# Attention and gated long convolution on one core: a new order for every engine's work, with higher planned costs for the shared-key loads

## The chip, the core and the metric

The kernel runs on one core of a Trainium2 chip. Its metric is the device time in microseconds, from the start of the program to its end. The three timed runs of the kernel before took 371.93, 372.42 and 373.16 us (median 372.42). A profile of one more execution was taken with the hardware profiler.

A core has five engines that each work through their own list of instructions: TensorE (PE, matmuls; its weight loads are listed apart as PEld), VectorE (DVE), ScalarE (ACT), GpSimd (POOL) and SyncE (SP, which here only issues transfers). An engine that waits for a semaphore holds up all that stands behind in its list.

## The reference

```python
def _attn_ref(q, k, v):                     # 8 batches, 12 heads, 448 rows, 64 wide
    scores = 1.0 / np.sqrt(64) * np.matmul(q, k.transpose(0, 1, 3, 2))
    m = np.max(scores, axis=-1, keepdims=True)
    e = np.exp(scores - m)
    attn = e / (np.sum(e, axis=-1, keepdims=True) + np.exp(-m) + 1e-09)
    return np.matmul(attn, v)

def _moe_ref(x, w_proj, filter_fft, w_out): # x [8, 448, 768]
    proj = x @ w_proj                       # three parts of 768: x1, x2, x3
    X2 = np.fft.rfft(x2, n=S, axis=1)
    H = np.fft.rfft(filter_fft, n=S, axis=0)[None, :, :]
    x2_conv = np.fft.irfft(X2 * H, n=S, axis=1)
    y = x1 * x2_conv * x3
    return y @ w_out
```

All inputs and the output, [8, 448, 768], are float32. The attention is a softmax whose sum has one more term; the kernel computes it as exp(s) / (sum of exp(s) + 1), with no maximum taken off, and the heads are laid side by side into x. The convolution is done with matmuls against tables of cosines and sines.

## The kernel before

**Attention.** Heads go in pairs, six per batch, 48 in all. For a pair, TensorE computes scores in 64x64 quarters of its array (`scores`, L947 and L952), three blocks of 128 keys per head, and a fourth of the last 64 keys of both heads (the "rests", loaded by `rests_load`, L509, in four transfers each for keys and values). ScalarE takes the exponentials (L966, into `e` or `er`). TensorE sums exponentials times values into a pair of PSUM banks (`out_rests` L977 for the rests, `out_rest` L997 for the others), and VectorE divides (L1010 to L1012, into `xb`). Queries and keys must be turned first: in batches 0 and 1 (`staged`) they are cast (L585, L591), turned by TensorE and evicted by ScalarE or VectorE through `copy` (L486 is ScalarE's line in it, L488 VectorE's); in batches 2 to 7 (`loaded`) GpSimd casts them (L733, L759) and transfers of SyncE turn them (`q_turn` L694, `k_turn` L705).

**The gated convolution** (`dense`), per batch: x is turned by a transfer (L1056); the projection gives x2 (L1175), which is turned back by a transfer (`turn2`, L1188); its spectrum (L1223), times the filter's (L1241), goes back through a matmul (L1319); the gate blocks `G` (L1273) project x1 and x3, and VectorE multiplies (L1288, L1361); the output blocks `O` (L1091) are evicted to a ring of three buffers `osb` (through `copy`, L486 or L488), two halves of 384 columns to a strip of 128 rows, and SyncE stores the strip (L1406; L1403 for a half). The tables `ft` and `fr`, with which spectra are taken, are made at the start (`weights`, L822 to L831, `ft` L870, `fr` L854 and L855).

**What sets the order.** The work of the whole program is a list of 2033 steps: 684 of TensorE, 378 of ScalarE, 579 of VectorE, 209 of GpSimd, 183 of SyncE. A step is `add(engine, cost, want, emit, need, make, take, give, ...)`: a planned cost, a function that issues its instructions, the tokens that it needs and makes, and the PSUM banks that it takes and gives back. `plan.ORDER` holds a rank for each step; an engine issues its steps in rising rank. `plan.FLIP` lists the evictions that go to the other engine of the pair ScalarE and VectorE. `Plan.run` (L91) then plays the program through with the planned costs, transfers shared between SyncE's and GpSimd's queue among them. From that come the PSUM bank of each step (`spots`; 8 banks, scores and sums take pairs) and the `fillers`, matmuls on an idle tile (L1566) that are put into the holes that it sees in the first 3 to 40 us, 47 of them here. Neither costs nor the played-through times are in the program itself; the chip only sees the order, the engines, the banks and the fillers. The fields of a transfer are its cost on the issuing engine, `dma` (its time on the DMA engines) and `run` (the length of its runs in the planner's count of descriptors); the constant `LANDING` is the planner's time from the end of a transfer to its landing.

```python
want = self.ORDER[len(self.tasks)] if self.ORDER else want + self.SHIFT.get(part, 0.0)
...
queue = {e: sorted(t for t in self.tasks if t[2] == e) for e in self.LAT}
...
def copy(e, to, of):
    if e == "ACT":
        nc.scalar.copy(to, of)
    else:
        nc.vector.tensor_copy(to, of)
```

## Time and profile before

| | |
|---|---|
| timed runs | 371.93, 372.42, 373.16 us; median 372.42 |
| span of the profiled execution | 370.8 us (its time outside the span is not in the profile) |
| TensorE busy | 356.4 us, 96% |
| VectorE busy | 274.8 us, 74% |
| ScalarE busy | 237.5 us, 64% |
| GpSimd busy | 127.6 us, 34% |
| transfers, share of 16 engines over the span | 61.6% SyncE's and ScalarE's queue, 25.4% GpSimd's |
| HBM read, written | 43.86 MB, 11.01 MB |

A row of the page's groups or of the timeline names line, engine, operation, and out<-in by the program's names. "PE psum L977 <- DVE osb L488" in the list of waits reads: matmuls of line 977 waited for VectorE's eviction into `osb`; then total us, times, longest. A row of the timeline has start and length in us, and in brackets the idle time of that engine just before and what ended it. "SPq" rows are transfers being issued by SyncE.

### The profile page before, as it was taken

The page shows a single profiled execution, that of the slowest core. Times are in us where ns is not written, and L with a number is a line of the kernel's source. Part 1 is how long each engine was busy: PE and PEld are TensorE (multiplying, and loading weights), DVE is VectorE, ACT ScalarE, POOL GpSimd, SP SyncE. Part 2 cuts the span into 40 slices and gives each one's busy share as a digit, 9 for nine tenths or more (in the row PEclk, how much of TensorE's full clock was granted, in tenths as well). Part 3 has the DMA queues.
Part 4 walks back from the last instruction along what each step waited for, and adds up shares of the span by engine and source line. Part 5 has one row for each costly group of instructions (what it writes and reads, how often), then busy time and mean ns, then how long its engine had stood idle before and what let it go on. Part 6 is the DMA issues. An engine that isn't in the chain of part 4 may idle for free. (4 is left out here: it accounts for less than half of the span.)

```text
span 370.8 us, 10707 instructions
## 1 busy us (share of the span) xinstructions
PE 356.4 (96%) x4300; PEld 211.8 (57%) x4300; DVE 274.8 (74%) x674; ACT 237.5 (64%) x379; POOL 127.6 (34%) x278
## 2 busy tenths in 40 slices
PE   7989999999999979999999999999999999999995
PEld 7666675554555545565555646665565655555552
DVE  5468659982789726897579977689459898779970
ACT  4999876756767548567565657867776561334343
POOL 9984251444625274265537523313100100000000
PEclk9999999999999999999999999999999999999999
DMA  9999999988999999999998799995830074125035
GB/s 169 194 191 204 207 207 205 206 169 160 168 242 156 229 214 208 235 242 192 206 182 202 166 245 192 262 208 122 171 72 1 7 196 89 42 45 170 4 129 172
DMA packets 133958, 61.93 MB, mean 167 GB/s; under 512 B 105165, under 2 KB 130704, under 8 KB 133904
## 3 DMA queue, kind: packets, MB, share of 16 engines
q1 hardware_dynamic: 111552, 48.71, 61.6%
q0 software_dynamic: 22112, 12.26, 25.4%
q8 instruction: 34, 0.56, 0.6%
q10 hardware_dynamic: 240, 0.23, 0.2%
q14 instruction: 20, 0.16, 0.2%
HBM read 43.86 MB, written 11.01 MB: 148 GB/s over the span
## 5 line engine op out<-in xcount | busy, mean ns | idle before, releaser
L966 ACT ACTIVATE e<-psum 128x896 bf16<-128x896 f32 x144 | 126.6, 920 | 40.8 <-PE psum L947 37.3
L1273 PE MATMUL psum<-xT,wproj_bf 128*128 128x448 bf16 x576 | 121.7, 353 | 0.1
L1273 PEld LDWEIGHTS <-wproj_bf 128*128 128x128 bf16 x576 | 53.4, 98 | 47.7 <-issue 5.0
L1091 PE MATMUL psum<-wout_bf,yT 128*128 128x384 bf16 x288 | 54.7, 326 | 0.8 <-DVE g L1288 0.4
L1175 PE MATMUL psum<-xf,wproj_bf 128*128 128x452 bf16 x252 | 53.9, 357 | 0.0
L947 PE MATMUL psum<-qT,kT 64*64 64x448 bf16 x576 | 45.4, 359 | 2.5 <-DVE g L1288 0.7
L997 PEld LDWEIGHTS <-e 128*128 128x128 bf16 x1152 | 42.0, 98 | 9.6 <-issue 5.2
L997 PE MATMUL psum<-vn,e 128*128 128x65 bf16 x1152 | 46.8, 194 | 0.0
L733 POOL CAST nat<-nat 112x512 bf16<-112x512 f32 x36 | 25.4, 708 | 44.7 <-DMA nat<-in_q_dram 41.8
L1241 DVE TENSOR_TENSOR t<-xs,hrs 113x768 bf16<-113x768 bf16 (+1 forms) x64 | 36.4, 578 | 2.9 <-ACT xs L486 2.3
L1288 DVE TENSOR_TENSOR g<-x,psum 128x448 bf16<-128x448 bf16 x48 | 29.2, 616 | 12.1 <-PE psum L1273 10.9
L1091 PEld LDWEIGHTS <-yT 128*128 128x128 bf16 x288 | 26.6, 98 | 19.9 <-issue 1.8
L1175 PEld LDWEIGHTS <-wproj_bf 128*128 128x128 bf16 x252 | 23.2, 96 | 22.2 <-issue 1.1
L486 ACT CAST x<-psum 128x448 bf16<-128x448 f32 (+1 forms) x39 | 20.4, 529 | 22.6 <-PE psum L1273 14.5
L759 POOL CAST nat<-nat 128x384 bf16<-128x384 f32 x36 | 21.5, 598 | 32.2 <-DMA nat<-in_k_dram 31.9
L486 ACT COPY osb<-psum 128x384 f32<-128x384 f32 x39 | 18.2, 486 | 20.1 <-PE psum L1091 15.9
L486 ACT CAST xs<-psum 113x384 bf16<-113x384 f32 (+1 forms) x41 | 19.2, 482 | 15.1 <-PE psum L1223 14.1
L1012 DVE TENSOR_TENSOR xb<-psum,den 128x896 bf16<-128x896 f32 x24 | 26.2, 1091 | 0.8
L486 ACT CAST cr<-psum 128x452 bf16<-128x452 f32 x35 | 18.0, 539 | 11.5 <-PE psum L1319 11.0
L947 PEld LDWEIGHTS <-kT 64*64 64x64 bf16 x576 | 15.6, 105 | 17.1 <-issue 12.9
L966 ACT ACTIVATE er<-psum 128x896 bf16<-128x896 f32 x24 | 22.2, 926 | 4.3 <-PE psum L952 3.5
L987 POOL MEMSET sinks<- 1x1 bf16 x18 | 1.6, 91 | 65.6 <-PE psum L977 65.6
(143 smaller groups left out, 501.3 us busy)
## 6 DMA issues: line engine op xcount, KB each, us to landing
nat<-in_q_dram SPq DMA_DIRECT2D x37, 224.0 KB, 3.8
out_dram<-osb SPq DMA_DIRECT2D x21, 384.0 KB, 3.5
nat<-in_k_dram SPq DMA_DIRECT2D x38, 192.0 KB, 3.9
nat<-in_v_dram POOLq DMA_DIRECT2D x15, 192.0 KB, 6.3
wproj_bf<-in_moe_w_proj_dram POOLq DMA_DIRECT2D x2, 1152.0 KB, 18.1
out_dram<-osb SPq DMA_DIRECT2D x12, 192.0 KB, 2.7
ks<-in_v_dram POOLq DMA_DIRECT2D x9, 192.0 KB, 4.9
rests<-in_k_dram SPq DMA_DIRECT2D x32, 48.0 KB, 4.3
```

Of the source, the lines that this page charges most:

```text
L486: nc.scalar.copy(to, of)
L733: lambda hp=hp, qsrc=qsrc: nc.gpsimd.tensor_copy(qn[:, hp].rearrange("p j (u d) -> p u j d", u=2), qsrc.rearrange("p (u j d) -> p u j d", ...
L759: lambda hp=hp, sv=sv: nc.gpsimd.tensor_copy(kn[:, hp // 2, 3 * (hp % 2) + 1 : 3 * (hp % 2) + 4].rearrange("p j (u d) -> p u j d", u=2), sv),
L947: nc.tensor.matmul(sc[r, u, 0:S], kT[b % 2][c, hp // 2, 3 * turned + t, r], qT[b % 2][c, hp, :])
L966: nc.scalar.activation(to, of, AF.Exp, scale=SCALE)
L997: nc.tensor.matmul(out_bank(u)[:, n + 3 * turned, :], P["e"][1 + t][:, o : o + 128], vn[b % 2][:, hp, 4 * u + t, :], start=False, stop=tur ...
L1012: nc.vector.tensor_tensor(W["xb", b][:, hp // 2].rearrange("p s (u d) -> p u s d", u=2), op[:, :, :, 0:DH], rec[:].unsqueeze(3).to_broadca ...
L1091: nc.tensor.matmul(ops[:n, :DCH], y[:, dt, 0:n], wout_bf[:, dt, ch * DCH : (ch + 1) * DCH], start=(dt == 0), stop=(dt == NDT - 1),)
L1175: nc.tensor.matmul(pps, wproj_bf[:, kt, D + dt * 128 : D + (dt + 1) * 128], W["xf", b][:, :, kt, 0:FQ], start=(kt == 0), stop=(kt == NDT - 1),
L1241: nc.vector.tensor_tensor(t[:K], L["xs", par, ch][:K], h, op=ALU.mult)
L1273: nc.tensor.matmul(p[:, :S], wproj_bf[:, kt, 2 * part * D + dt * 128 : 2 * part * D + (dt + 1) * 128], xT()[:, kt, 0:S], start=(kt == 0), ...
L1288: nc.vector.tensor_tensor(g[:, dt, :], L["x1", dt], p[:, :S], op=ALU.mult)
```

## The change

The diff has four parts. Two constants of the planner: `LANDING` from 1.89 to 1.85, and a new `COLL`, which is 0.0 and with that value delays nothing in the planner's transfers. Costs: the loads of the shared keys and values (`rests_load`) from 2.5 or 2.6 to 2.9 or 2.95 of SyncE and from 1.2 or 1.25 to 1.75 (keys) or 1.4 (values) of the DMA engines; `turn2` from 1.65 to 1.75; and `run` from 0.2 to 30 for all turning transfers. A new `plan.ORDER`. A new `plan.FLIP`, in which 129 steps change engine (ScalarE has 381 steps after it, VectorE 576). The steps themselves, their shapes, tiles and rings are the same. After the planner's class the lines of the new file are higher by 8.

```diff
-    LANDING = 1.89
+    LANDING = 1.85
...
+    COLL = 0.0
...
+                if len(heads) == 2 and heads["SP"][2][15] and heads["POOL"][2] is not met:
+                    met, stall = heads["POOL"][2], clock + self.COLL
                     continue
...
-    plan.ORDER = (9, 0, 6, 1370, 8, 10, 1, 5, 13, 18, 20, 11, 68, 120,
+    plan.ORDER = (4, 2, 13, 1316, 9, 11, 1, 6, 10, 18, 22, 7, 19, 181,
...
-    plan.FLIP = (30, 49, 71, 87, 94, 98, 376, 378, 380, 438, 464,
+    plan.FLIP = (29, 30, 38, 55, 71, 72, 75, 86, 93, 97, 98, 378, 384, 388, 437, 463,
...
-                    add("SP", 2.6, want + (0.05 if name == "k" else SLOT[0] + 0.05) if b == 0 else want - RE1 + 0.1 * n,
+                    add("SP", 2.9, want + (0.05 if name == "k" else SLOT[0] + 0.05) if b == 0 else want - RE1 + 0.1 * n,
...
-                        dma=1.25, run=22, begun=[("ir", b)], n=4)
+                        dma=1.75 if name == "k" else 1.4, run=22, begun=[("ir", b)], n=4)
...
-            add("SP", 2.5, tau(i0) - lead[0] - 0.2 + 0.1 * n,
+            add("SP", 2.95, tau(i0) - lead[0] - 0.2 + 0.1 * n,
...
-                need=[("cr" + name, b - 1)], make=[("r" + name, b)], dma=1.2, run=22, n=4)
+                need=[("cr" + name, b - 1)], make=[("r" + name, b)], dma=1.75 if name == "k" else 1.4, run=22, n=4)
...
-                    make=[("qT", i) for i in gs], dma=(0.7, 1.43)[few > 1], run=0.2, late=-0.2, turn=True)
+                    make=[("qT", i) for i in gs], dma=(0.7, 1.43)[few > 1], run=30, late=-0.2, turn=True)
...
-                add("SP", 1.65, w - 2.0, lambda: turn2(ch), need=[("x2s", b, d) for d in range(dt - 2, dt + 1)],
+                add("SP", 1.75, w - 2.0, lambda: turn2(ch), need=[("x2s", b, d) for d in range(dt - 2, dt + 1)],
```

What the tables do to the order is shown at two places. The first is the start of the program, before the first scores. On VectorE the kernel before makes the rows `edge`, `half` and `jm` (of `weights`), then casts the first queries (`ldm` from `nat`), makes the table `ft` and casts the first keys:

```order
L805 SCALAR_TENSOR_TENSOR ph_183<-rd_188,ph_183 128x452
L822 TENSOR_SCALAR edge_214<-row_180 128x1
L823 TENSOR_SCALAR e2_215<-row_180 128x1
L824 TENSOR_TENSOR edge_214<-edge_214,e2_215 128x1
L826 TENSOR_SCALAR half_219<-edge_214 128x1
L829 TENSOR_SCALAR back2_221<-row_180 128x1
L831 TENSOR_SCALAR jm_223<-ci_130,back2_221 128x113
L591 CAST ldm_106<-nat_105 112x2x4x64
L870 TENSOR_SCALAR ft_83<-sb_225,half_219 113x452
L585 CAST ldm_106<-nat_105 128x2x3x64
```

The changed kernel has there, on VectorE:

```order
L813 SCALAR_TENSOR_TENSOR ph_194<-rd_199,ph_194 128x452
L599 CAST ldm_106<-nat_105 112x2x4x64
L830 TENSOR_SCALAR edge_219<-row_191 128x1
L831 TENSOR_SCALAR e2_220<-row_191 128x1
L832 TENSOR_TENSOR edge_219<-edge_219,e2_220 128x1
L834 TENSOR_SCALAR half_224<-edge_219 128x1
L837 TENSOR_SCALAR back2_226<-row_191 128x1
L839 TENSOR_SCALAR jm_228<-ci_130,back2_226 128x113
L878 TENSOR_SCALAR ft_83<-sb_215,half_224 113x452
L872 TENSOR_SCALAR bt_85<-psum_115,half_224 113x113
L875 COPY bt_85<-psum_115 113x339
L593 CAST ldm_106<-nat_105 128x2x3x64
```

The cast of the queries now stands ahead of the six rows of `weights`, and the table `bt`, which stood behind the cast of the keys and three evictions of keys and queries, ahead of that cast. ScalarE's first evictions at the same place, of the kernel before (`kT` are turned keys, `fr` the second table, `e0` to `e2` exponentials of pairs 0 and 1):

```order
L1579 ACTIVATE warm_122<-zero1_121 128x1
L486 COPY kT0_89<-psum_115 128x384
L966 ACTIVATE e1_97<-psum_115 128x2x448
L966 ACTIVATE e0_96<-psum_115 128x2x448
L854 CAST fr_84<-psum_115 113x452
L855 ACTIVATE fr_84<-psum_115 113x226
L966 ACTIVATE e2_98<-psum_115 128x2x448
```

And of the changed one, on ScalarE:

```order
L1587 ACTIVATE warm_122<-zero1_121 128x1
L862 CAST fr_84<-psum_115 113x452
L863 ACTIVATE fr_84<-psum_115 113x226
L494 COPY qT0_91<-psum_115 128x448
L494 COPY kT0_89<-psum_115 128x384
L974 ACTIVATE e0_96<-psum_115 128x2x448
L974 ACTIVATE e1_97<-psum_115 128x2x448
L974 ACTIVATE e2_98<-psum_115 128x2x448
L494 COPY kT0_89<-psum_115 128x384
```

`fr` has moved from behind two exponentials to the front, and the first turned queries (`qT`), which VectorE evicted, come to ScalarE. The second place is near 130 us, where batch 0's second output strip is stored while batch 2's keys and queries are loaded. SyncE's list there, of the kernel before (`nat` are loads, `osb` is the strip, `rests` the shared values):

```order
L705 DMA_TRANSPOSE kT1_90<-nat_105 128x10x128
L727 DMA nat_105<-in_q_dram 112x2x256
L747 DMA nat_105<-in_k_dram 128x2x192
L1406 DMA out_0_dram<-osb_1732 128x768
L509 DMA rests_104<-in_v_dram 64x3x64 x4
```

And of the changed kernel, on SyncE:

```order
L713 DMA_TRANSPOSE kT1_90<-nat_105 128x10x128
L702 DMA_TRANSPOSE qT1_92<-nat_105 128x12x112
L755 DMA nat_105<-in_k_dram 128x2x192 x2
L1414 DMA out_0_dram<-osb_1842 128x768
L755 DMA nat_105<-in_k_dram 128x2x192
L735 DMA nat_105<-in_q_dram 112x2x256 x2
L517 DMA rests_104<-in_v_dram 64x3x64 x4
```

Of the loads and turns around the store, one key load has gone from ahead of it to behind it, and the shared values stand three loads further back. VectorE's list at the same place, of the kernel before, where the copies into `osb` are those of batch 1's strips 0 and 1:

```order
L1012 TENSOR_TENSOR xb_2575<-psum_115,den1_108 128x2x7x64
L1361 TENSOR_TENSOR yR_1599<-g_1906,cv_2483 128x2x64
L1288 TENSOR_TENSOR g_2600<-x1_2491,psum_115 128x448
L488 COPY osb_2606<-psum_115 128x384
L488 COPY osb_2592<-psum_115 128x384
L488 CAST x1_2667<-psum_115 128x448
L488 CAST x1_2693<-psum_115 128x448
```

And of the changed kernel, on VectorE, where the one copy is that of strip 1:

```order
L1020 TENSOR_TENSOR xb_2613<-psum_115,den1_108 128x2x7x64
L1296 TENSOR_TENSOR g_2627<-x1_2444,psum_115 128x448
L496 COPY osb_2656<-psum_115 128x384
L496 CAST ldm_106<-psum_115 128x4x113
L1054 TENSOR_TENSOR low_109<-low_109,den0_107 128x42
L496 CAST x1_2705<-psum_115 128x448
L1018 TENSOR_SCALAR den1_108<-psum_115 128x14
```

Strip 0's copies are now ScalarE's, ahead of this place, and one copy is left on VectorE. In PSUM, the sums of pair 10 (`out_rests`) take banks 0 and 1 instead of 6 and 7, and the gate block `G(2, 1, 0)`, which follows on TensorE, takes bank 7, which that copy frees. Between 93 and 103 us TensorE's list has the output block of six matmuls, which followed batch 1's last spectral projection (L1175), ahead of that and the one before; SyncE's list up to the transfer `turn2` behind it has the same rows in the same order. There are 72 fillers in the first 40 us instead of 47, and without the fillers TensorE's list changes 158 times between quarter-array and full-array matmuls, where it changed 164 times.

More of the change, by code (lines that the diff above doesn't have):

```diff
@@ L115, in run @@
         landed = {"SP": [], "POOL": []}
+        stall, met = -1.0, None
         def done(t, end, by):
@@ L167, in soonest @@
             if over() > 1e-9 and queues["SP"][0] in heads and queues["SP"][0][2][15]:
-                soon = soon + [clock + over() * total / queues["SP"][0][2][11]]
-            return max(min([clock + h[1] * total / h[2][11] for h in heads] + soon), now + 1e-6)
+                soon = soon + [max(clock, stall) + over() * total / queues["SP"][0][2][11]]
+            return max(min([max(clock, stall) + h[1] * total / h[2][11] for h in heads] + soon), now + 1e-6)
         def spots(t):
@@ L765, in loaded @@
                         add("SP", (1.3, 1.8)[few > 1], tau(g) - lead[2], lambda hp=hp: k_turn(hp), need=[("ck", i) for i in gs] + ([("crk", b)] if few > 1 or hp % 2 == 0 else []) + last,
-                            make=[("kT", i) for i in gs], dma=(0.4 + 0.095 * (block(hp + few) - block(hp))), run=0.2, late=-0.2, turn=True)
+                            make=[("kT", i) for i in gs], dma=(0.4 + 0.095 * (block(hp + few) - block(hp))), run=30, late=-0.2, turn=True)
                 else:
@@ L1079, in attention @@
                 add("SP", 2.5 if hp == 3 else 1.3, w, x_dma, need=[("xb", NHP * b + h) for h in ps] + old,
-                    make=[m for h in ps for m in (("X", NHP * b + h), ("xT", b, h))], dma=1.55 if hp == 3 else 0.8, run=0.2, late=-0.2, turn=True)
+                    make=[m for h in ps for m in (("X", NHP * b + h), ("xT", b, h))], dma=1.55 if hp == 3 else 0.8, run=30, late=-0.2, turn=True)
         else:
```

12 lines of the change are left out of this document (8 added, 4 removed).

## Prediction

> **What bounds the kernel now.** I read the page first, then who waited on TensorE, then a table of five stretches, and last the order of time around the longest waits. The page gives the span and each engine's busy time.
>
> ```profile
> span 370.8 us, 10707 instructions
> ...
> PE 356.4 (96%) x4300; PEld 211.8 (57%) x4300; DVE 274.8 (74%) x674; ACT 237.5 (64%) x379; POOL 127.6 (34%) x278
> ```
>
> TensorE works for all but 14.4 us of the span. Both versions issue the same matmuls apart from fillers, so the change can move only those 14.4 us and the small losses between matmuls. The table of stretches says where the idle time lies (busy us and number of instructions per engine, then the granted clock, the DMA share and GB/s).
>
> ```profile
> 10.00:40.00 30.00, 27.73 (x556) 19.18 (x557) 20.95 (x58) 28.74 (x46) 20.59 (x42) 1.00 1.36 197
> 40.00:100.00 60.00, 59.09 (x762) 35.34 (x759) 41.56 (x96) 41.70 (x67) 26.42 (x56) 1.00 1.08 192
> 100.00:140.00 40.00, 36.19 (x463) 20.70 (x461) 28.99 (x70) 25.33 (x38) 18.83 (x42) 1.00 1.15 203
> 140.00:360.00 220.00, 219.37 (x2397) 126.56 (x2396) 177.30 (x431) 132.91 (x215) 52.53 (x112) 1.00 0.73 150
> ```
>
> TensorE idles 2.27 us in 10 to 40, 0.91 in 40 to 100, 3.81 in 100 to 140, and only 0.63 in the 220 us after that. In 10 to 40 ScalarE is the fuller engine, 28.74 of 30. So the first 40 us hang on ScalarE and on arriving data, and the rest is TensorE with a few holes. The waits on TensorE name them (total us, times, longest).
>
> ```profile
> PE psum L977 <- DVE osb L488: 2.5, 2, 2.3
> ...
> PE psum L1223 <- DMA x<-ldm: 0.8, 1, 0.8
> ...
> PE psum L947 <- DVE g L1288: 0.7, 2, 0.5
> ...
> DVE osb L488 <- DMA out_dram<-osb: 3.8, 1, 3.8
> ```
>
> The first row is the big hole, and the last one is its cause, as the order of time shows (start, length, engine, line, and in brackets the idle time before).
>
> ```profile
> 124.72 0.41 SPq L1406 DMA_DIRECT2D out_dram<-osb  x1
> 125.17 2.75 SPq L509 DMA_DIRECT2D rests<-in_v_dram  x4
> ...
> 129.45 0.57 PE L947 MATMUL psum<-qT,kT 64*64 64x448 bf16 x8
> ...
> 131.66 1.02 DVE L488 COPY osb<-psum 128x384 f32<-128x384 f32 x2 [3.81 <-DMA out_dram<-osb]
> ...
> 132.27 0.19 PE L977 MATMUL psum<-vn,er 64*64 64x65 bf16 x1 [2.25 <-DVE osb L488]
> ...
> 132.73 0.29 PE L977 MATMUL psum<-vn,er 64*64 64x65 bf16 x13 [0.28 <-DVE osb L488]
> ```
>
> The store of batch 0's second strip is issued at 124.72. It lands so late that VectorE, which wants its buffer, starts the copy of batch 1's strip only at 131.66. That copy and the next one free banks 6 and 7, which the sums of pair 10 (`out_rests`, L977) take. TensorE stands for 2.25 + 0.28 = 2.53 us.
>
> **The change, part by part.** New values in `Plan` (`LANDING`, `COLL`, costs of `rests_load`, `run`) reach the chip only through order, banks and fillers. Four places carry the sum.
>
> *The store at 125 us.* In the new order ScalarE copies batch 1's first strip early, and pair 10's sums take banks 0 and 1, which an exponential frees. The store still stands in the way: VectorE's copy of strip (1, 1) waits for it, and now the gate matmul `G(2, 1, 0)`, next on TensorE after the sums, takes bank 7 that this copy frees. VectorE's queue behind the copy holds an eviction of `x2h`, an `x1` and the next `xb`, so they wait too. One 192 KB key load has moved from ahead of the store to behind it; the pace of 125 to 130 us is the nearest row.
>
> ```profile
> 125.00:130.00 5.00, 5.00 (x39) 2.40 (x38) 2.75 (x7) 3.03 (x6) 0.65 (x2) 1.00 1.09 225
> ```
>
> At 225 GB/s that is 0.85 us, so the copy would start at 131.66 - 0.85 = 130.8 and end half of 1.02 later, at 131.3. TensorE had finished the scores at 129.45 + 0.57 = 130.02; by the new order about 0.8 us more of work (sums and shifted blocks) precedes `G(2, 1, 0)`, so it asks at 130.8. Of 2.53 us some 0.5 remain: **-2.0 us**, bounds -2.5 (the store lands in time) and 0 (it lands as late as before and TensorE comes earlier).
>
> *Changes between quarter-array and full-array matmuls.* Their price stands in the stretch before 103 us, read on TensorE, with two rows of SyncE's queue and, first, the gate matmuls' group on the page (busy us, mean ns of one).
>
> ```profile
> L1273 PE MATMUL psum<-xT,wproj_bf 128*128 128x448 bf16 x576 | 121.7, 353 | 0.1
> ...
> 91.66 1.92 PE L1175 MATMUL psum<-xf,wproj_bf 128*128 128x452 bf16 x9
> ...
> 93.97 1.14 PE L1091 MATMUL psum<-wout_bf,yT 128*128 128x384 bf16 x6
> ...
> 97.18 1.30 PE L1273 MATMUL psum<-xT,wproj_bf 128*128 128x448 bf16 x6
> 98.41 0.38 PE L947 MATMUL psum<-qT,kT 64*64 64x448 bf16 x4
> ...
> 99.29 2.44 PE L1273 MATMUL psum<-xT,wproj_bf 128*128 128x448 bf16 x12
> ...
> 102.98 0.53 PE L1223 MATMUL psum<-x,ft 113*113 113x384 bf16 x2 [0.81 <-DMA x<-ldm]
> ...
> 94.69 0.41 SPq L727 DMA_DIRECT2D nat<-in_q_dram  x1
> 95.21 1.84 SPq L1188 DMA_TRANSPOSE x<-ldm  x1
> ```
>
> Twelve gate matmuls last 2.44, the last one its mean 0.353 of it, so their pitch is 2.09 / 11 = 0.19. Six from 97.18 should end their turn at 98.32, but the 64*64 scores start at 98.41: 0.09 us for one change of shape. Leaving fillers out, the old order has 164 such changes and the new one 158, so **-0.5 us** (0 where a wait swallows it). The Trainium skill, "TensorEngine Tiling (Array Packing)", section Key Properties, says that changing the tiling mode drains TensorE; it gives no figure, and by it alone the term would have this sign and no size. The trace agrees, with 0.09.
>
> *The transposed x2 of batch 1.* In those rows the last spectral projection ends at 93.58, and TensorE comes for the transposed result at 102.98 - 0.81 = 102.17 and waits 0.81. The new order puts the output block of 93.97 (6 matmuls of 384 columns, 6 x 0.19 x 384 / 448 = 0.98) ahead of both projections: TensorE comes 0.98 sooner after the last of them. If the transfer keeps its distance from the projection, the wait grows to 1.79 (+0.98). If it keeps its place in SyncE's queue, whose rows up to it are in the same order and where the row before was issued just 0.5 us earlier, it grows less (0). I take **+0.5**, halfway. SyncE has the query and key turns of batch 3 behind this transfer, so they shift with it.
>
> *The start.* VectorE now casts the first queries ahead of the six small `weights` operations, and ScalarE evicts `fr` and the queries ahead of the first keys.
>
> ```profile
> 1.09 4.11 PE L1574 MATMUL psum<-idle 128*128 128x128 bf16 x38 [1.09 <-DVE one L1478]
> ...
> 3.88 0.15 DVE L822 TENSOR_SCALAR edge<-row 128x1 f32<-128x1 f32 x1
> ...
> 4.57 0.31 DVE L831 TENSOR_SCALAR jm<-ci,back 128x113 bf16<-128x113 int32 x1
> ...
> 5.15 0.71 DVE L591 CAST ldm<-nat 112x512 bf16<-112x512 f32 x1 [0.27 <-DMA nat<-in_q_dram]
> ...
> 6.35 0.61 PE L1566 MATMUL psum<-idle 128*128 128x128 bf16 x8
> ...
> 7.59 0.48 ACT L486 COPY kT<-psum 128x384 bf16<-128x384 bf16 x1 [1.49 <-PE psum L624]
> ...
> 8.12 0.57 PE L947 MATMUL psum<-qT,kT 64*64 64x448 bf16 x8 [0.34 <-ACT kT L486]
> ...
> 10.36 0.54 ACT L854 CAST fr<-psum 113x452 bf16<-113x452 f32 x1
> ...
> 10.93 0.36 ACT L855 ACTIVATE fr<-psum 113x226 bf16<-113x226 f32 x1
> ```
>
> The cast waits for its load whatever its place, so it ends at 5.86. `weights` (3.88 to 4.88, 1.0 us) sat in that wait and now follows, to 6.85; then `ft` (0.3), TensorE's mirror matmul at 7.2 to 7.5, `fr` on ScalarE (10.36 to 11.29, 0.93) to 8.5, the queries' copy (about 0.5) and the keys' (0.48) to 9.4. The first scores start at 9.4 instead of 8.12: 1.25 late. ScalarE also takes five more evictions of keys and queries (11 listed in `FLIP` against 6), 5 x 0.48 = 2.4 us in a stretch where it had 1.3 free. What covers this is other TensorE work pulled forward: two filter matmul pairs and a key turn before pair 2's last sums, and the gate blocks before the projections. The gate weights are now loaded ahead of the others.
>
> ```profile
> 23.16 0.82 POOL L924 DMA_DIRECT2D wproj_bf<-in_moe_w_proj_dram  x1
> ...
> DMA to landing us min/median/max: 10.3/14.1/21.9
> ```
>
> Issued about 2 us earlier, at 21, and 14.1 later there, they are in at 35; by the durations above TensorE reaches the first gate block at about 35. The bounds of this place are 0 (the old waits and its 47 fillers of about 0.055 us, which do nothing, take up the delay) and 1.25 + 2.4 = 3.7. The first is nearer, since the stretch to 40 us holds 2.3 us of waits and 2.6 of fillers: **+0.3**.
>
> *All else.* Every stretch is reordered, but from 40 to 100 and 140 to 360 there are only 0.91 + 0.63 = 1.5 us to gain, and an order of the same quality has about as many again: **0**, bounds -1.5 and +1.5. The end is alike: the last block, its eviction and its store.
>
> ```profile
> 366.56 0.48 ACT L486 COPY osb<-psum 128x384 f32<-128x384 f32 x1 [0.45 <-PE psum L1091]
> 367.07 0.33 SPq L1403 DMA_DIRECT2D out_dram<-osb  x1
> ```
>
> The sum is -2.0 - 0.5 + 0.5 + 0.3 = **-1.7 us**: a span of 369.1 instead of 370.8. The profile gives that execution's span alone, no time around it. The timed runs have a median of 372.42, 1.62 above the span; with the same 1.62 the forecast is **370.7 us**.
>
> **The rivals.** *The store's wait only changes its place.* For it: VectorE's copy still stands behind the store, and TensorE asks bank 7 back within 1 us of the old time. Against: a key load less ahead of it, and half the hand-over gone. With 0.7 won instead of 2.0 the time is 372.0, no change.
>
> *The start is not covered (slower).* Place: TensorE's first gate block at about 35 us. If its weights land later, or ScalarE's load keeps the sums of pair 2 back, the whole 3.7 us arrive instead of 0.3: 370.7 + 3.4 = 374.1. It decides from a delay of 3.1 us at that block on, which gives 373.5. For it: ScalarE at 28.74 of 30; the planner itself sets 72 fillers where it set 47, that is, it sees more holes. Against: the work pulled forward.
>
> *The slow pace of the matmuls returns.* The 38 matmuls at 1.09 take 4.11 us, 0.107 each, the fillers at 6.35 (0.61 - 0.22) / 7 = 0.056: half pace at first, while the clock column says 1.00. If a quiet stretch in the new start brings that back for another 4 us, about 2 us of work are lost: 372.7. The Trainium skill, "TensorE: Matmul & The Clock Gate", "Part 1: The HAM clock gate", has the array at half clock until it was busy for a window of about 3.4 us, and again after an idle one. Against it stands the 2.25 us hole at 132, behind which gate matmuls run at full pace, and the fillers.
>
> *All holes shrink.* If the small waits go too, as -1.5 for all else, the time is 369.2.
>
> **How the numbers follow.** About 0.3%, 1.1 us, is what a measurement of this kernel tells from no change, so faster is below 371.3 and slower above 373.5. Forecast 0.46, all holes shrink 0.09: faster 0.55. Store wait moved 0.23, slow pace 0.05: same 0.28. Start not covered 0.17: slower. The range runs from 368.9, a little below the case of all holes, to 373.4, which leaves out most of the slower case and little else. The forecast's own range is 369.6 to 371.3.
>
> **What would show it.** Right: no wait on a VectorE `osb` copy above 1 us around 130, 100 to 140 idle about 2 us less, the first scores near 9.4, a wait of 0.8 to 1.8 for the transposed x2 near 103, and TensorE's 10 to 40 busy within 1 us of 27.7. Wrong: the first gate block later than 36 us, waits of over 2 us in 140 to 360, or a VectorE copy that still starts after 131.5.

## The result and the profile after

The changed kernel is slower. Its median is 375.93 us over 20 runs (373.23 to 378.9) against 372.18 us for the kernel before over 20 runs (370.07 to 376.44), a ratio of 1.0099 with a 95% interval of 1.0073 to 1.0125: some 3.7 us lost where 1.7 were forecast as won. Ratios leave out the few executions more than 1.5% above the fastest of their kernel, medians do not. A repeat on another chip gave 375.56 against 372.74, 1.0076 (1.0041 to 1.0111). The profiled execution took 378.63 us, with a span of 376.9; it is one of the slowest, so its own losses are larger than the usual ones.

The page of the changed kernel, span and busy time:

```profile
span 376.9 us, 10764 instructions
...
PE 360.2 (96%) x4325; PEld 212.7 (56%) x4325; DVE 276.0 (73%) x671; ACT 240.4 (64%) x382; POOL 126.8 (34%) x278
```

TensorE is idle for 16.7 us instead of 14.4, and busy for 3.8 us longer with the same matmuls and 25 more fillers, which follow each other at 0.056 us. The stretches, in the columns of the prediction, say where.

```profile
10.00:40.00 30.00, 27.42 (x544) 18.78 (x542) 21.95 (x58) 26.57 (x43) 20.53 (x41) 1.00 1.35 196
40.00:100.00 60.00, 59.22 (x788) 35.96 (x780) 42.67 (x99) 42.17 (x65) 23.96 (x50) 1.00 1.04 178
100.00:140.00 40.00, 37.60 (x465) 21.52 (x463) 30.16 (x71) 25.66 (x39) 19.16 (x41) 0.96 1.13 208
140.00:360.00 220.00, 216.84 (x2376) 123.58 (x2375) 171.33 (x413) 135.22 (x219) 53.88 (x117) 0.99 0.73 150
```

Between 100 and 360 us the granted clock is below 1, which it was not before; from 40 to 100 us the transfers move 178 GB/s where they moved 192; and 140 to 360 has 3.2 us of idle time where it had 0.63. The list of waits on TensorE, of the changed kernel, has two long ones:

```profile
PE psum L1231 <- DMA x<-ldm: 2.4, 1, 2.4
PE psum L1281 <- DVE ldm L496: 2.4, 1, 2.4
```

The first is the turned x2 of batch 1, which the forecast put at 0.81 plus 0.5. The second was not there before: an eviction of batch 2's next projections waits for the single buffer that the turn of the first half still reads. The wait for the store at 132 us, the largest before, is gone: `G(2, 1, 0)` starts without one. The order of time of the changed kernel, from the last turns of batch 1 to the first long wait:

```profile
51.05 1.55 POOL L522 CAST nat<-rests 64x384 bf16<-64x384 f32 x2 [7.88 <-PE psum L637]
...
51.25 0.36 PE L650 MATMUL psum<-ident_bf,nat 112*64 112x112 bf16 x8
...
52.66 0.61 POOL L741 CAST nat<-nat 112x512 bf16<-112x512 f32 x1
...
53.30 2.21 SPq L702 DMA_TRANSPOSE qT<-nat  x1
...
95.62 3.59 SPq L517 DMA_DIRECT2D rests<-in_k_dram  x4
...
100.47 2.75 SPq L1196 DMA_TRANSPOSE x<-ldm  x1
...
102.56 1.31 PE L1281 MATMUL psum<-xT,wproj_bf 128*128 128x448 bf16 x6
...
106.27 0.99 PE L1231 MATMUL psum<-x,ft 113*113 113x384 bf16 x3 [2.40 <-DMA x<-ldm]
...
108.74 3.03 PE L1281 MATMUL psum<-xT,wproj_bf 128*128 128x448 bf16 x12
```

In the kernel before, the last turn of queries (L650, there L642), the first cast of queries and the first turning transfer stood earlier:

```profile
47.12 0.36 PE L642 MATMUL psum<-ident_bf,nat 112*64 112x112 bf16 x8
...
49.36 0.82 POOL L733 CAST nat<-nat 112x512 bf16<-112x512 f32 x1 [1.87 <-DMA nat<-in_q_dram]
...
50.21 1.32 SPq L694 DMA_TRANSPOSE qT<-nat  x1
```

TensorE's last turns of batch 1 (pairs 10 and 11) free the buffers that GpSimd's first casts of batch 2 write, and these casts give SyncE its first turning transfer. All three are 3 to 4 us later. In the kernel before the turns were done 2 us ahead, and the cast waited last for its own load, 1.87 us; in the changed kernel the load is there, and GpSimd stands 7.88 us for the turns (4.55 before). Part of the delay is GpSimd's own order: the changed kernel makes two casts of shared keys (1.55 us) ahead of the first cast of queries, the kernel before one (0.51). SyncE then issues with few gaps, and 45 us on the turn of x2 is issued at 100.47 instead of 95.21. Twelve gate matmuls behind the wait take 3.03 us; before they took 2.44. The clock by stretches, of the changed kernel:

```profile
104.00:106.00 2.00, 0.00 (x0) 0.00 (x0) 0.18 (x1) 0.51 (x2) 1.48 (x4) 1.00 1.07 211
106.00:108.00 2.00, 1.74 (x20) 1.44 (x21) 0.92 (x2) 0.96 (x2) 1.52 (x5) 0.63 1.00 203
108.00:110.00 2.00, 2.00 (x16) 1.15 (x14) 1.45 (x4) 0.48 (x1) 0.00 (x0) 0.52 1.20 160
```

A wait of 2.40 us is followed by two stretches of 2 us whose mean clock is 0.63 and 0.52, (0.37 + 0.48) x 2 = 1.7 us lost besides the wait. It is the same behind the second:

```profile
137.59 1.94 SPq L1196 DMA_TRANSPOSE x<-ldm  x1
...
143.77 0.63 DVE L496 CAST ldm<-psum 128x452 bf16<-128x452 f32 x1 [2.93 <-DMA x<-ldm]
...
144.45 2.40 PE L1281 MATMUL psum<-xT,wproj_bf 128*128 128x448 bf16 x6 [2.35 <-DVE ldm L496]
```

Six gate matmuls take 2.40 us here, where six took 1.30 before. The end, of the changed kernel:

```profile
371.61 1.16 SPq L1417 DMA_DIRECT2D out_dram<-osb  x2
371.79 0.48 ACT L494 COPY osb<-psum 128x384 f32<-128x384 f32 x1 [0.80 <-PE psum L1099]
372.87 0.52 SPq L1411 DMA_DIRECT2D out_dram<-osb  x1
```

The last store starts 0.60 us after the end of its eviction at 372.27, since SyncE is still issuing two others. In the kernel before two others stood ahead of it as well, but were through at 366.72, and it started 0.03 us after its eviction:

```profile
365.41 1.31 SPq L1403 DMA_DIRECT2D out_dram<-nat  x2
```

### The profile page after: what moved, and what is told of

Same layout as the page of the kernel before. It is cut to its first block, busy times and chain, and to the rows that moved or that the text cites. A ratio compares the mean times of both kernels' runs of the same rounds, so it can differ in the third digit from the quotient of the medians.

```text
span 376.9 us, 10764 instructions
## 1 busy us (share of the span) xinstructions
PE 360.2 (96%) x4325; PEld 212.7 (56%) x4325; DVE 276.0 (73%) x671; ACT 240.4 (64%) x382; POOL 126.8 (34%) x278
## 5 line engine op out<-in xcount | busy, mean ns | idle before, releaser
L1281 PE MATMUL psum<-xT,wproj_bf 128*128 128x448 bf16 x576 | 123.5, 356 | 2.4 <-DVE ldm L496 2.4
L1183 PE MATMUL psum<-xf,wproj_bf 128*128 128x452 bf16 x252 | 55.0, 358 | 0.0
L1005 PE MATMUL psum<-vn,e 128*128 128x65 bf16 x1152 | 48.2, 195 | 0.0
L494 ACT COPY osb<-psum 128x384 f32<-128x384 f32 x42 | 19.7, 486 | 20.3 <-PE psum L1099 20.2
L767 POOL CAST nat<-nat 128x384 bf16<-128x384 f32 x36 | 19.7, 558 | 38.6 <-DMA nat<-in_k_dram 38.5
L1255 DVE TENSOR_TENSOR yh<-t 112x384 bf16<-112x384 bf16 (+1 forms) x64 | 23.5, 387 | 0.3
L494 ACT CAST cr<-psum 128x452 bf16<-128x452 f32 x29 | 15.4, 546 | 11.0 <-PE psum L1327 9.7
```

The lines of the kernel that those rows point to most:

```text
L1005: nc.tensor.matmul(out_bank(u)[:, n + 3 * turned, :], P["e"][1 + t][:, o : o + 128], vn[b % 2][:, hp, 4 * u + t, :], start=False, stop=tur ...
L1183: nc.tensor.matmul(pps, wproj_bf[:, kt, D + dt * 128 : D + (dt + 1) * 128], W["xf", b][:, :, kt, 0:FQ], start=(kt == 0), stop=(kt == NDT - 1),
L1255: nc.vector.tensor_tensor(yh[:K, par, n, ch * DCH : (ch + 1) * DCH], t[:K, 0, :], t[:K, 1, :], op=(ALU.subtract, ALU.add)[n],)
L1281: nc.tensor.matmul(p[:, :S], wproj_bf[:, kt, 2 * part * D + dt * 128 : 2 * part * D + (dt + 1) * 128], xT()[:, kt, 0:S], start=(kt == 0), ...
```

## The experiments

A theory and its rivals came from these rows. *The late queue*: SyncE's list starts 3 us late and stays late, and TensorE pays in waits, some with the slow pace behind them. Its first form was only "the two waits". Rivals: *the start* costs the time by itself; *many small losses*; *the planner's by-products* (other banks, more fillers). `T 10` and `T 11` below are the two turns; an entry of `ORDER` is the rank of a step on its engine. All ratios are to the kernel before on the same chip.

**Fillers in the two waits.**

```diff
+full.update({1142: 36 matmuls on the idle tile ahead of it, 1295: 36 ahead of it})
```

> The changed kernel with 36 matmuls on the idle tile put ahead of the first spectrum of batch 1's second half (the 2.40 us wait at 106 us) and 36 ahead of the gate block that waits 2.35 us at 144 us; 36 x 0.056 is 2.0 us each. Nothing else differs. Theory of the two waits: behind both waits TensorE runs at half pace for about 3.5 us (12 gate matmuls 3.03 us instead of 2.3, granted clock 0.52 to 0.63), so a wait costs itself plus about 1.7 us; the idle matmuls leave the waits but keep the pace, so the clock column shows 1.00 behind them, and the time falls by up to 3.4 us, to about 373 to 374, less where an execution has only one such wait. Theory of the start: the reordered first 60 us cost the time, and this changes nothing: 376. Theory of many small losses: nothing or 1 us slower, 376 to 377.

Measured 379.2, 1.0167 (1.0132 to 1.0201): slower than the changed kernel. Its profile:

```profile
104.57 2.17 PE L1577 MATMUL psum<-idle 128*128 128x128 bf16 x36
...
108.13 2.43 PE L1284 MATMUL psum<-xT,wproj_bf 128*128 128x448 bf16 x12
...
369.31 0.82 PE L1102 MATMUL psum<-wout_bf,yR 128*128 128x384 bf16 x4 [1.39 <-issue]
```

The pace behind them was full (2.43 for twelve, against 3.03), as the theory said. The gain did not come, and the time lies above all three expectations. Why is not shown: the fillers may cost more than the waits in executions where these are short, and 1.39 us of waiting for "issue" came in the last blocks, inside a group of matmuls, which no other profile here has there. So this says how the pace hangs on the wait, and nothing on the sum.

**Work moved ahead of the two waits.**

```diff
-ORDER[1170], ORDER[1160], ORDER[1295], ORDER[1265] = 616, 621, 815, 848
+ORDER[1170], ORDER[1160], ORDER[1295], ORDER[1265] = 597.33, 599.67, 801.33, 801.67
```

> The changed kernel with two gate blocks (2.3 us) moved on TensorE ahead of the first spectrum of batch 1's second half, and two others moved ahead of the last spectral projections of batch 2, so that TensorE has work where it waited at 106 and 144 us. Theory of the two waits: both waits go or fall below 0.5 us, the granted clock stays 1.00 there, and the time falls by 4 to 7 us, to about 369 to 372. Theory of the start: 375 to 376, for the waits are taken up later. Theory of many small losses: 375.

Measured 377.09, 1.0131 (1.0088 to 1.0175). Both waits were gone in its profile, and the time was not better: the theory of the two waits falls in its first form. Instead TensorE waited 1.64 us at 96 us for the turn of x2's first half, so to fill one wait moved the next one up.

**Halves of the two orders.** The planner's own times cut the list: all steps that one order starts before 60 us, then the rest by the other.

```diff
-plan.ORDER = new
+plan.ORDER = [old[i] - 100000 if i in started_before_60 else new[i] for i in steps]
```

> Order and engines of the kernel before for every step that the planner starts in its first 60 us, those of the changed kernel for the rest (banks and idle matmuls planned anew). Theory of the two waits: they lie behind 100 us and stay, so the time is 374 to 376, at most 1.4 us below the changed kernel. Theory of the start: the loss goes, 371 to 372.5. Theory of many small losses: in between, 374.

> The other way round: order and engines of the changed kernel for every step that the planner starts in its first 60 us, those of the kernel before for the rest. Theory of the two waits: the wait for the store at 132 us is back and the two new ones are gone, so the time is that of the kernel before plus up to 1.4 us, 372.5 to 374. Theory of the start: 375 to 376. Theory of many small losses: 373 to 374.

Measured 375.61, 1.0088 (1.0056 to 1.012), with the old start, and 375.3, 1.0064 (1.0032 to 1.0096), with the new one. Neither theory had both slow, and the two losses are 1.5% together, where the whole new order loses 1.0%: those of two halves of a searched order need not add.

**The planner's by-products.** First the new file with the old tables:

```diff
-plan.ORDER, plan.FLIP = new
+plan.ORDER, plan.FLIP = old
```

> The changed file with the kernel before's ORDER and FLIP, so the new planner constants and costs alone: the instructions of every engine stand as in the kernel before, 188 of 535 PSUM places and the idle matmuls (67 instead of 47) differ. Theory of the planner's by-products: the parts so far (each half of the new order alone was slower by 0.6 to 0.9% with these idle matmuls and banks) share these, so this is slow too, 375 to 376. Theory of the order: the loss lies in the tables, so this runs as the kernel before, 372 to 373.

Then the kernel before with the new tables:

```diff
-plan.ORDER, plan.FLIP = old
+plan.ORDER, plan.FLIP = new
```

> The kernel before with the new ORDER and FLIP, but its old planner constants and costs: the order of the changed kernel, with 181 of 535 PSUM places and 68 instead of 72 idle matmuls. Theory of the planner's by-products: 372 to 373.5. Theory of the order: as the changed kernel, 375 to 377.

And the changed kernel without fillers:

```diff
-    FILL = (3.0, 40.0, 0.6)
+    FILL = (0.0, 0.0, 0.6)
```

> The changed kernel without any idle matmuls after the first 38. Theory of the planner's by-products, in the form that idle matmuls delay real work: 72 x 0.056 = 4.0 us less to do, so up to 3 us faster, 373 to 374. Theory of the order: the holes that they filled stay, and the early matmuls may fall back to half pace for some us: 376 to 378.

Measured 372.91, 0.9987 (0.9946 to 1.0028); 375.39, 1.0073 (1.0033 to 1.0114); 375.36, 1.0058 (1.0017 to 1.0099). The loss lies in the tables. Without fillers the granted clock of its timed runs fell to a mean of 0.984, which is worth 6.0 us of the span, and yet the time stayed: 72 fillers buy about as much pace as they cost (an estimate from 72 x 0.056 = 4.0 us and the change of clock, 3.8 us).

**The kernel before again.**

> The kernel before once more, for a second profile of it: if the first 10 us and the wait for the store at 132 us differ by a microsecond or more from the first profile, single profiles can't place differences of that size.

One run of 372.59 us, span 370.7. Its waits on TensorE:

```profile
PE psum L1223 <- DMA x<-ldm: 1.8, 1, 1.8
PE psum L1574 <- DVE one L1478: 1.1, 1, 1.1
```

The wait for the store, 2.5 us in the first profile, is not in this list at all, and that for the turned x2 is 1.8 instead of 0.8. The same instructions in the same order have either of two waits, by the execution.

**The late transfer taken forward, then with the old end.**

```diff
-ORDER[1119] = 563
+ORDER[1119] = 533.0
```

> The changed kernel with the transfer that turns batch 1's second half of x2 moved on SyncE ahead of the four loads of batch 3's shared keys and two further loads. Theory of the late queue: with the new order SyncE's list runs 3 to 4 us behind from 53 us on, the turned x2 lands some 3 us too late, and TensorE loses about 2 us more than before around 105 us in every profile of the new order; here the wait goes and the time falls by about 2 us, to 374. Rival, the loss only moves on: the loads put behind come 3 us later and hold up the turns of batch 3, 375.5 to 376.5.

> The same, and from the planner's 250 us on the order and engines of the kernel before. Every profile of the new end has 5.0 to 5.1 us between TensorE's last matmul and the end of the span, every one of the old end 4.2 to 4.3. Theory of the late queue with the end as second loss: 0.8 us less than the kernel above, 373.2 if that takes 374. Rival, the end costs nothing: the same as the kernel above.

Measured 377.64, 1.0148 (1.0099 to 1.0197), and 378.59, 1.0162 (1.0121 to 1.0203). The turn of x2 is issued at 97.65 and nobody waits for it, but from the profile of the first:

```profile
109.33 0.31 PE L985 MATMUL psum<-vn,er 64*64 64x65 bf16 x14 [0.91 <-POOL sinks L995]
...
110.61 0.57 PE L955 MATMUL psum<-qT,kT 64*64 64x448 bf16 x8 [0.97 <-DMA kT<-nat]
```

The turned keys of batch 3, put behind it, are what comes late now (3.31 us of wait in the profile of the second). The loss only moves on, as the rival had it, and both times lie above the 375.5 to 376.5 that the rival gave.

**The store moved ahead in the kernel before.**

```diff
-ORDER[1084] = 722
+ORDER[1084] = 639.5
```

> The kernel before with the store of batch 0's second strip moved ahead on SyncE, right behind that of the first strip, some 15 us earlier; the strip is ready at 95.6 us. The wait behind that store was 2.53 us in the first profile and nothing in the second. Theory of the late queue: the wait goes for good, which is worth its mean over executions, about 1.2 us: 371.2. Rival, the wait was a chance of one execution: no change, 372 to 373.

Measured 372.43 against 373.13, 0.9985 (0.9951 to 1.0019), no change by the interval. The whole store wait, 2.53 us in the profile that the prediction read, is worth 0.6 us in the mean, and perhaps nothing.

**Only the middle of the new order.**

```diff
-plan.ORDER = new
+plan.ORDER = [new[i] if 60 <= started[i] < 250 else old[i] + (1e5 if started[i] >= 250 else -1e5) for i in steps]
```

> The kernel before up to the planner's 60 us and from its 250 us on, the changed order only between. Theory of the late queue (the loss begins before 60 us) with the end as second loss: 372 to 373, as the kernel before. Rival, the middle costs time as well: 374 to 375.

Measured 376.35, 1.0126 (1.0075 to 1.0176): the expectation missed. This third mixture is no faster than the whole new order, and clearly slower than the old one, so mixtures at seams can't split the loss. What was left was to move single steps.

**The last turns of batch 1, late in the kernel before and early in the changed one.** The six entries are the two turns and their evictions.

```diff
-ORDER[92], ORDER[96] = 267, 269
+ORDER[92], ORDER[96] = 294.33, 295.67
```

> The kernel before with the last two key and query turns of batch 1 on TensorE (pairs 10 and 11), and their evictions, moved about 5 us back, behind 5 us of projections, as in the changed order. GpSimd's first cast for batch 2 needs them, and SyncE's first turning transfer needs that cast. Theory of the late queue: the first turning transfer is issued at 53.5 to 54.5 instead of 50.2 to 51.5, SyncE's list runs 3 us later up to 100 us, the turned x2 of batch 1 lands after 105, and the time rises by about 2 us to 374.5. Rival, the lateness is taken up by slack in the list and the loss of the new order comes from elsewhere: 372 to 373.

```diff
-ORDER[92], ORDER[96] = 284, 288
+ORDER[92], ORDER[96] = 258.67, 259.33
```

> The changed kernel with the same two turns and their evictions moved about 5 us ahead, in front of two projections. Theory of the late queue: the first turning transfer is issued at about 51 to 51.5 instead of 53.3 to 54.6, the turned x2 lands about 2 us earlier, and the time falls by 1.5 to 2 us, to 374. Rival: no change, 375.5 to 376.

Late in the kernel before: 373.2, 1.0035 (0.9999 to 1.007). Its profile:

```profile
52.65 1.33 SPq L694 DMA_TRANSPOSE qT<-nat  x1
...
95.63 2.11 SPq L1188 DMA_TRANSPOSE x<-ldm  x1
...
105.82 0.53 PE L1223 MATMUL psum<-x,ft 113*113 113x384 bf16 x2 [3.08 <-DMA x<-ldm]
```

The first turning transfer came at 52.65, less late than expected, with GpSimd's one cast ahead of it as before. SyncE had caught up by the turn of `x` (L1056), whose issue ended at 66.70 against 66.13. So the turn of x2 was issued as early as before. Yet it landed at 105.8, later than the 102.1 to 104.6 of four profiles of the old order, and TensorE waited 3.08 us. The time lies between the theory's 374.5 and the rival's 372 to 373, and is not clear of no change. Early in the changed kernel: 375.43, 1.0064 (1.003 to 1.0097), with the first turning transfer at 51.6, the issue of the turn of `x` over at 66.18 instead of 69.78, and the turned x2 in at 103.2 instead of 106.2. So the queue went by the theory, but the time by the rival: no change against the changed kernel. The turns are done at 47.2 there, and what comes last is again the load:

```profile
50.94 0.61 POOL L741 CAST nat<-nat 112x512 bf16<-112x512 f32 x1 [3.22 <-DMA nat<-in_q_dram]
```

So turns that come 4.4 us earlier bring the transfer forward by 1.7. From 50 to 70 us the transfers of the kernel before, the changed one, and the changed one with early turns moved:

```profile
50.00:70.00 20.00, 19.54 (x285) 12.68 (x278) 17.49 (x41) 14.47 (x25) 6.72 (x12) 1.00 1.24 195
```

```profile
50.00:70.00 20.00, 19.93 (x303) 12.56 (x302) 18.21 (x44) 13.33 (x23) 7.57 (x14) 1.00 1.11 164
```

```profile
50.00:70.00 20.00, 19.32 (x276) 12.27 (x273) 16.45 (x41) 12.68 (x20) 6.97 (x12) 1.00 1.19 195
```

The last column is GB/s: 195, 164, 195. That is 0.62 MB in 20 us, or 3.2 us of transfers at 195 GB/s, by which the changed kernel is behind, and the early turns bring it back. The kernel before with the late turns moves 195 in its profile as well, so late turns alone don't cost this; the order around them has a part in it.

**The new end alone.**

```diff
-plan.ORDER = old
+plan.ORDER = [old[i] if started[i] < 250 else new[i] + 1e5 for i in steps]
```

> The kernel before up to the planner's 250 us, the changed order from there. Theory that the new end costs 0.8 us: between TensorE's last matmul and the end of the span lie 5.0 to 5.1 us instead of 4.2 to 4.3, and the time is 373.2 to 373.7. Rival, nothing: 372.5.

Measured 373.07, 1.003 (0.9993 to 1.0066). Its end:

```profile
366.07 1.36 SPq L1417 DMA_DIRECT2D out_dram<-osb  x2
366.25 0.48 ACT L494 COPY osb<-psum 128x384 f32<-128x384 f32 x1 [0.81 <-PE psum L1099]
367.53 0.52 SPq L1411 DMA_DIRECT2D out_dram<-osb  x1
```

The two stores are again ahead of the last one, which starts 0.80 us after its eviction, and 5.15 us lie between the last matmul and the end of the span, as in the changed kernel (5.10) and not as before (4.30). These are 4.97 to 5.15 us in all 11 profiles with the new end and 4.13 to 4.75 in the nine with the old one. The time alone is not clear of no change.

**Both put in, both taken out, and the changed kernel again.**

```diff
-kernel before
+kernel before with the late turns and the new end
```

> The kernel before with both losses put in: batch 1's last turns late as in the kernel with late turns, and the changed order from the planner's 250 us on. Alone they cost 1.1 and 1.2 us in the mean (intervals down to nothing). Theory of the late queue and the end: they add up, about 2.2 us, 374.5. Rival, both were scatter: 372.5 to 373.

```diff
-changed kernel
+changed kernel with the early turns and the old end
```

> The changed kernel with both losses taken out: batch 1's last turns early, and the order of the kernel before from the planner's 250 us on. Theory of the late queue and the end: 2 us less than the changed kernel on the same chip, about 374, of which 1.5 us above the kernel before stay unexplained. Rival, mixtures are slower whatever they hold: 375.5 to 377.

> The changed kernel once more, on the chip of the two mixtures and for a second profile of it: 375.5 to 376.5, a first turning transfer at 53.3 to 54.6 us, 5.0 to 5.1 us from TensorE's last matmul to the end of the span; the waits of 2.4 us at 106 and 144 us need not be there again.

On one chip, against 372.74: 374.69, 1.0054 (1.0018 to 1.0091), with both put in; 375.14, 1.0045 (1.0007 to 1.0082), with both taken out; 375.56, 1.0076 (1.0041 to 1.0111), for the changed kernel. The two together slow the kernel before by 2.0 us, with an interval that leaves out no change. Taking them out wins 1.2 us by the ratios, where 2 were expected, and that difference is not clear of scatter. With both taken out the first turning transfer came at 51.84 and the turn of x2 was issued at 99.27 all the same (99.32 in the repeated profile of the changed kernel), so an early start of the list does not by itself bring that turn back. In the repeated profile of the changed kernel the wait at 106 us was 1.25, and the one behind the single buffer was there again:

```profile
143.35 1.29 PE L1281 MATMUL psum<-xT,wproj_bf 128*128 128x448 bf16 x6 [2.86 <-DVE ldm L496]
```

This time the six matmuls behind it took 1.29 us, full pace.

Each timed run lists its granted clock. Over the 105 runs of the kernel before beside these experiments that the ratios use, its mean is 0.9976 (mean time 372.67), over 30 of the changed one 0.9945 (375.91). Run by run, (1 - clock) x span is 0.90 us and 2.06 us in the mean. So of the 3.2 us between these two means about 1.2 are lost pace, and 2 are everything else.

## Why the prediction was wrong, step by step

*The store, -2.0.* The place was right, and the wait did go. The step that failed is its size: 2.53 us was taken from one execution as if every one had it. A second profile has none, and moving the store is worth 0.6 us (interval -0.7 to 1.8).

*The start, +0.3, and its cover.* The rows up to the first scores came about as forecast: the first scores at 8.83 (forecast 9.4, before 8.12). The first gate block came at 36.47, later than the 36 that the prediction had named as a sign of being wrong, though earlier than before (38.77). The step that failed is the cover. TensorE's 10 to 40 us looked alike, 27.42 busy against 27.73, but fillers count as busy. Of the kernel before and of the changed one, the fillers alone in that stretch:

```profile
10.00:40.00 30.00, 1.96 (x17) 1.11 (x17) 1.00 1.36 197
```

```profile
10.00:40.00 30.00, 3.42 (x42) 2.46 (x42) 1.00 1.35 196
```

Without them TensorE worked 25.77 us before and 24.00 after, so some 1.8 us of work were behind at 40 us where 0.3 were booked (an estimate, since busy times of matmuls overlap; counted by columns, as below, it is 1.0 in this pair). And the sum did not follow the two turns that had moved 4 us back on TensorE to GpSimd and SyncE, which wait for them. What the late turns cost alone is not clear of nothing (1.3 us, 0.0 to 2.6). The rival "start not covered" had the sign and about half the size (374.1, 1.7 us above before, where 3.7 were measured), but its place, a late gate block, was wrong.

*The turned x2, +0.5 between 0 and 0.98.* The argument "it keeps its place in SyncE's queue, whose rows up to it are in the same order" failed: the rows are the same, but the queue reaches them late. It was issued at 100.47, not 95.21, and at 99.32 in the second profile, not 95.89. How much of this is the late start is open, by the runs with the turns moved. The wait grew from 0.81 to 2.40 in the first pair of profiles; in the second it shrank from 1.8 to 1.25, so there the loss lay elsewhere. Putting only the late turns into the kernel before brought a wait of 3.08 us at this place.

*All else, 0 between -1.5 and +1.5.* From 140 to 360 us TensorE idles 3.16 us in the first profile of the changed kernel and 3.42 in the second, where the kernel before idled 0.63 and 1.77. A wait of over 2 us there, a sign of being wrong by the prediction, came in both. But two more profiles with the new tables, one in the kernel before and one without fillers, have 1.09 and 0.25: this stretch scatters by more than the bound, which was read from one execution.

*The end, nothing.* "The end is alike" was wrong by 0.8 us: the same last block, eviction and store, but two stores of another strip (L1417), which came earlier in SyncE's list before, stand directly ahead of the last one and hold it up. The size is seen in every profile with the new end, while the timed runs with that end alone leave no change open.

*The slow pace, given 0.05.* It returned, not at the start but behind waits. It costs about 1.2 us more in the mean than before. The Trainium skill, "TensorE: Matmul & The Clock Gate", section "HAM oscillation — how this bites in real kernels", has the array fall to half clock when a wait crosses a window of about 3.4 us. Here 2.40 and 2.35 us were enough and 2.25 (the store of the kernel before), 2.86 and 3.08 were not, so a wait below that figure can cost pace, in some executions and not in others. That the hole at 132 us had cost none, which the prediction held against this rival, was luck of where it fell (last section).

*The changes of shape, -0.5.* No run separates it, and its 0.09 us for one change was read at one place.

*The interval.* The range ended at 373.4. Scatter between executions, 370.1 to 376.4 us of one kernel, was not in it, and the terms were all read from one of them. No luck hid an error here: the store, the start, the end and the pace were all off the same way.

What stays open is some 1 to 2 us of the loss. The late turns and the new end together account for 2.0 us (0.7 to 3.4) when put into the kernel before, and for about 1.2 when taken out of the changed one. That a mixture of two orders costs time whatever it holds is not ruled out. The wait behind the single buffer at 142 to 145 us, 2.35 and 2.86 us in the two profiles of the changed kernel, may be the rest: it is there with the early turns and the old end too (2.30). Against it, no such wait stands in the profiles with the new tables in the kernel before and without fillers, whose medians are only 0.2 to 0.6 us lower, and moving gate blocks ahead of both waits won nothing. Nothing was tried on it alone.

Where the loss arises can be estimated by counting TensorE's matmuls by their columns, without fillers and those of quarters as a quarter. Three profiles with the new tables (two of the changed kernel, one of the kernel before with them) are behind four with the old ones by 1.3 us at 40 us, 1.2 at 100, 3.0 at 110, 3.5 at 160 and at 360, and 4.4 at the end. So it comes in four pieces, the start, the turned x2, the place of the single buffer, and the end.

## What to carry to other kernels

Where a moved step frees a buffer or feeds a cast, follow it through every engine to the first transfer that waits for it, and on to the next place where that queue stands anyway: a start 2.4 us late was made up there in one kernel, and one 3 us late was not in another. Take fillers out of a busy time before calling a delay covered. Before a wait is booked as a gain, look for it in a second profile; one execution's 2.5 us was worth 0.6. And where transfers are behind as a whole, filling or reordering one wait only shows the next.

## What the runs showed of the hardware

The same four instructions of VectorE at 1.47 us took 0.92 us in the kernel before, and 2.43 in the kernel with the old start and the new rest, which has them in the same place:

```profile
1.47 0.92 DVE L794 TENSOR_SCALAR ph<-ci,row 128x113 f32<-128x113 int32 x4
```

```profile
1.47 2.43 DVE L802 TENSOR_SCALAR ph<-ci,row 128x113 f32<-128x113 int32 x4
```

In the second, GpSimd's memsets beside them took 0.15 to 0.20 us each, in the first 0.22 to 0.31. With the new start and the old rest, and in the repeated profile of the changed kernel, it was `ft` that stood beside GpSimd's casts, where the first profile of the changed kernel has it at 0.49 us:

```profile
6.12 1.76 DVE L878 TENSOR_SCALAR ft<-sb,half 113x452 bf16<-113x452 bf16 x1
```

So the start of one program scatters by 1.3 us with one instruction. The Trainium skill, "SBUF — State Buffer", section "SBUF: two separate sides", says that VectorE and GpSimd share a pair of ports by an exclusive lock: for a GpSimd instruction, or one of VectorE in a mode of two ports, whichever starts first has it for its whole length, and the other is blocked. The rows fit this, but no run here separates it from other causes.

What sets waits that cost pace apart from those that don't can be read from the traces. The granted clock in them is 1.00 or 0.50, never between, and until the last matmuls every stretch of 0.50 behind the first rise of the clock begins a whole number of 3.41 us behind that rise and lasts 3.41 us, or three times that without fillers. Laid out in such windows, the changed kernel around its wait of 2.40 us, then its second profile around that of 2.86 us (window, its length, TensorE busy; the clock is third from the end):

```profile
103.11:106.53 3.42, 1.02 (x6) 0.43 (x5) 1.07 (x4) 1.40 (x3) 2.01 (x5) 1.00 1.25 236
106.53:109.94 3.41, 3.41 (x32) 2.29 (x31) 2.31 (x5) 1.44 (x3) 0.99 (x4) 0.50 1.07 165
```

```profile
138.41:141.82 3.41, 2.08 (x16) 0.74 (x15) 0.81 (x1) 1.84 (x3) 0.00 (x0) 1.00 1.42 173
141.82:145.23 3.41, 1.88 (x10) 0.97 (x10) 1.18 (x2) 0.54 (x1) 2.25 (x7) 1.00 0.91 266
145.23:148.64 3.41, 3.41 (x61) 2.23 (x60) 0.63 (x2) 2.30 (x4) 2.21 (x5) 1.00 1.07 247
```

The first wait lies in one window, 2.40 us idle of 3.42, and the next window runs at half pace. The second, though longer, is cut by a boundary into 1.33 and 1.53 us, and costs none. Over the 20 profiles seven windows with 1.85 to 3.31 us idle were each followed by one at half, and with up to 1.78 us idle none was, but for one: without fillers 1.55 us, in the window from 6.10, was enough. So a wait of some 2 to 3 us cost pace or not by where it fell.
